# Another order table for a two-stage attention kernel: the same 3969 steps issued in another order, in other banks and buffers

## The chip, the cores and the metric

The kernel runs on one core of one Trainium2 chip. The metric is the device time of one execution in microseconds (us); the program is one launch.

## The reference, cut to what matters

Stage one is clustered attention over 4 batches of 8 heads, 768 positions, 64 values a head. Each query and each key belongs to the nearest of 16 centroids, and a query sees only the keys of its own cluster. Stage two takes the result as x (4 x 768 x 512), and runs causal attention with 4 experts of 64 values each; of an expert's output each token takes the share that its gate gives to that expert if it is one of the token's best two.

```
mask = q_assign[:, :, :, None] == k_assign[:, :, None, :]
scores = where(mask, q @ k.T / 8, -1e9);  attn = softmax(scores);  x = attn @ v
for e in range(4):
    a = softmax(causal((x @ wq[e]) @ (x @ wk[e]).T / 8))
    out += gate_e * (a @ (x @ wv[e]) @ wo[e])
```

## The kernel before

Work is cut into 24 pairs. Pairs 0 to 15 are pairs of heads of stage one, pairs 16 to 23 are pairs of experts of stage two, two for each batch. For each pair the kernel makes operands (`attention_operands` or `moe_operands`), and then runs `core`: scores once to find the maximum of each row (L975 on TensorE, read by VectorE at L983 and L985), the maxima turned into a row (L1001 on TensorE, copied at L1007, placed by a small transfer `tq<-mr`), the scores once more, with the maximum taken off, as two matmuls that add up (L1058 and L1059), the exponential on ScalarE (L1064), the weighted sum of values (L1102), and the sums of the exponentials (partial sums on VectorE or GpSimd, L381 and L382, then L1126).

Three sets of operand tiles `tk` and `tq` go round, so that operands are made ahead. Operands reach them by transfers (`put`, `place_rows`), all issued from one queue, SyncE's (SP below; every such instruction has line L369). For a pair of stage one the last of them are the cluster rows (`tq<-rows`, `tk<-rows`), which leave when the step at L607 is done, and the scaled queries: L648 multiplies out the scale on TensorE, VectorE applies it (L660), ScalarE makes the rounded half (L376), and the transfer `tq<-hi` carries it. The first L975 of that pair waits for them.

Before the first three pairs can be filled, GpSimd clears the three sets (`clear_rows`, four memsets each, L464 and L465: steps 64, 246 and 414).

At the start of each batch of stage two, `x_parts` loads x in four parts (`vt<-x` or `vm<-x`), rounds each (`xh`, L376 or L377) and takes the rest (`xl`, L381 or L382). The projections (L761) need all four. The loads of batches 1 to 3 use two buffers `vt` in turn, so a load waits for the `xl` step of the load before it in the same buffer.

What runs when is not decided by these functions: they only list steps. `SEQ` is a table of step numbers, and `run` issues the steps in that order; the letters a, d and p move a step to ScalarE, VectorE or GpSimd, where it has such a second way. `SLOT` says for each tile which buffer it gets, `ps` being the eight banks of TensorE's results.

```
for word in SEQ.split():
    i = int(word.rstrip("adp"))
    o = self.ops[i]
    eng = self.LETTER.get(word[-1], o.eng)
    ...
    o.ways[eng][1]()
```

So each engine, and the SP queue, works through its own steps in the order in which they stand in `SEQ`, and waits at a step until what that step needs is there. Nothing behind it on the same engine or queue gets past.

Steps that the text names, by their number in `SEQ`:
- 40, 49, 222 and others at L513: loads of q, k and v; 2274 and 2265 are the q and k of pair 13, 1945 the v of pair 11
- pair 0 and 1: 44 (a rounding rest on GpSimd), 260 (scaled queries, `tq<-xl`), 248 and 247 (cluster rows)
- pair 12: 2131 (the second L648), 2135 (`tq<-hi`), 2167 (first L975)
- pair 15: 2630 (the second L648), 2688 and 2643 (L975 of that pair)
- batch 2 of stage two: 3370, 3373, 3376, 3379 (the four loads), 3372 and 3375 (`xl` of the first two), 3377 (`xh` of the third), 3240 and 3241 (`tq<-hi`), 3242 (`tq<-lo`), 3385 (an L761 step that needs all four parts)
- the end: 3935 (sums, L893 and L895), 3894 and 3937 (L908), 3925 (L1102)

The table also holds 37 steps (0 to 36) of two matmuls without use, which stand in the first 20 us.

Of the kernel before, what the change touches and what calls it, by code (L numbers as in the profile page):

```python
# [10 lines left out]
def _warn_once_fixed(msg, *args, **kwargs):  # L11
# [34 lines left out]
422 310 195 268 145 306 177 184 423p 307 196 271 308 185 191 309 263 200 192 272 186 426 264 300 207 187 428 427p  # L46
311 288 189 303 180 190 175 289 202 181 429 269 301 197 203 182 270 208 292 265 183 205 293 261 198 298 188 266 285
201 277 281 206 286 559 283 278 296 560 251 279 273 282 194 193d 274 199 299 297 294 570 284 275 571 210 276 204 561
295 312 280 287 209 211 313 468 563 314d 469 456 315 462 476 457 568 572 441 564d 458 569 178 430 459 212 463 573
179d 477 574 330 442 565 320 213 470 584 445 335 471 353 446 336 575 354 349 576 734 331 332 350 322 214 321 363  # L50
566p 325 364 453 355 323 454 562p 464 318 356 577 351 333 316 326 466 465 358 317 337 319 370 215 359 324 578 338
586 437 579 342 371 438 460 352 451 360 467 343 580 452 361 443 357 585 439 581 327 440 373 328 444 472 587 374 433
473 907 365 329 340 434 366 583 449 447 461 341 474 368 588 725 435 478 369 450 375 582 362 591 431 589 432 376 378
592 436 334 593 448 216 217 590 595 455 475 345 594 596 367d 479 372 480 379d 339 346 481 627 639 482 635 628 483
618 735 636 612 730 736 597 377 640 737 731 619 602 643 732 726 644 738 598 629 218 727 526 603 344 538 728 613 495
527 630 488 539 751 600 599 616 489 610 625 631 611 641 493 642 404 740 494 617 929 347 626 741 380 601 219 381 620
632 614 496 623 742 348 624 528 220 382 637 615 521 638 604 729p 498 522 605 519 499 543 621 520 733p 536 743 523
537 508 524 645 541 509 606 383 529 517 744 542 533 753 518 503 544 531 646 525 484 532 745 752 504 608 746 486 485
633 747 534 634 500 530 748 490 607 510 750 609 758 934 511 647 622 754 938 491 384 505 535 487 755 648 385 546 506
759 760 649 492d 756 501 762 761 935d 497d 650 513 757 749 502d 763 540d 507d 386 547d 512d 514 787 739 651 810 790  # L60
652 695 791 675 696 788 806 930 936 807 665 931 1096 792 811 771 932 775 892 939 666 388 776 800 676 705 764 772 940
767 657 545 706 768 808 653 658 801 783 688 906 793 690 689 784 802 955 941 691 809 773 654 667 774 662 942d 798 956
677 663 803 655 678 708 799 668 794 804 656 670 795 1105 709 779 659 777 671 781 660 778 765 780 672 661 785 796 673
786 515 664 548 797 944 766 782 945 769 812 549d 686 387 770 946 687 805 680 516 937p 947 550 933p 813 957 814 948
789 551 949 815 700 950 816 710 681d 817 701 951 669d 684 952 703 1101 711 953 958 674 704 698 959 962 893 693 963
1097 389 694 824 552 685 839 964d 960 827 692d 840 822 966 820 825 862 828 965 823 697d 863 954 821 1098d 961p 699
713 967 702d 553 707 968 714d 1016 842 1017 1012 221 832 843 679 1013 994 1102 1004 844 995 833 985 1099 1005 834
1103 979 829 845 980 712 1123 991 1014 830 855 1015 875 856 992 983 818 876 904 986 973 835 1104p 996 1108 984 1263
1106 1109 997 870 554 819 998 1107d 987 871 853 826 988 975 872 999 977 851 978 682 852 974 715 873 1111 683d 716
976 854 717 831d 877 1112 969 857 970 1008 1010 858 1444 1002 1113 1011 989 556 971 1009 1006 837 1114 838 847 1100p  # L70
878 836 1124 990 1007 1115 1122 555 1003 972 859 1116 1272 981 1117 1000 865 982 1118 993 867 1001 1119 860 841 1018
1268 1121 861 1125 1019 848 1129 1020d 1120 866 1130 868 880 1126 1021 1131d 1127 718 1132 864d 1133 1128 869d 1041
943 874d 1048 1042 1057 1269 1273 719 879 1058 1031 881d 720 1049 1026 1038 1134 1027 1022 1032 1064 1274 846d 1161
1046 1023 1135 1076 1065 1181 1039 1024 1182 1047 1055 1162 1275 1077 721 1173 1025 1059 1174 1167 1036 1060 1168
1165 1276 1071 1166 1056 1152 1264 1072 1153 1169 1148 1266 1430 1033 1270d 1265 1138 1170 1043 1290 1034 1271p 1028
1149 1037 1278 1044 1029 882 1289 1279 723 849 883d 1139 850 1150 1142 1280 1151 1267p 1136 884 1179 1281 1144 1051
1030 1145 1143 722 1282 1035 885 1180 1137 1291 1154 1283 1155 1183 1061 1284 1146 1069 1062 1184 1439 1285 1147
1063 1158 1286 1079 1159 1163 1081 1070 1287 1052d 1292 1080 1296 1164 1066 1082 1288 1074 1293 1067 1431 1297 1075
1171 1068 1175 1294 1177 1172 1140 1298 1156 1432d 1435 1300 1084 1157 1176 1299p 1178 1301 1185 886 1295p 1141 1160
1073 887 1085d 1186 1442 1187 1040 1440 1188 1443 1350 1305 1441d 1436 1340 1336 1306 1346 1437 1445 1351 1433 1078  # L80
1347 1456 1446 1334 1338 1341 1315 1191 1337 1215 1192 1335 1313 1083 1213 1302 1339 1210 1214 1447 1314 1216 1243
1316 1211 1189 888 1448 1319 1045 1317 1190 1228 1244 1233 1229 1200 1110 1246 1201 1449 557 1231 1050 1234 1193
1457 1205 1194 1318 1203 1247 1224 1204 1450 1438p 1226 1225 1451 1238 1206 1320 1303 1232 1325 1434p 1241 1304 1239
# [136 lines left out]
    vt="011011110101010100101001010101",  # L220
    mx="0110100110100101101010010110100101010101",
# [1071 lines left out]
```

## Time and profile before

| | |
|---|---|
| median of three executions | 693.67 us |
| lowest and highest | 691.22 and 694.33 us |
| profiled execution: its own time | 696.02 us |
| profiled execution: span, first to last instruction | 694.3 us |
| mean granted TensorE clock | 0.997 of full speed |

Busy time is a share of the span. The span is 1.7 us shorter than the time of the execution. The profiled execution is 2.35 us above the median.

### The profile page before, as it was taken

Reading aid. Unit: us, or ns where it says so; the run is one execution under the profiler, and the core shown is the slowest. Engines: PE = TensorE matmul, PEld = TensorE weight load, DVE = VectorE, ACT = ScalarE, POOL = GpSimd, SP = SyncE. Lnnn points to the kernel's source line nnn. Section 1 sums busy time; section 2 is a strip of 40 time slices with the busy share of each in tenths; the row PEclk is TensorE's granted clock in tenths of the full one; section 3 lists DMA queues with packets and bytes.
Section 4 is the critical chain, followed back from the end, with each engine's and each line's share of the span. In section 5 each row is a group of like instructions: output and inputs, shape, how many; then the busy total and the mean of one; then the engine's idle time right before and its main releaser. Section 6 shows DMA issues by size and latency. Waiting matters only on the chain.

```text
span 694.3 us, 13123 instructions
## 1 busy us (share of the span) xinstructions
PE 678.3 (98%) x4529; PEld 526.0 (76%) x4529; DVE 537.1 (77%) x1216; ACT 348.4 (50%) x866; POOL 337.0 (49%) x283
## 2 busy tenths in 40 slices
PE   7999999999999999999999999999999999999997
PEld 5767677767767767757767688779868988887776
DVE  7988899899889798889898865875766476567643
ACT  4646466545646646647656632543443245233542
POOL 4776755555866685664798552110323424122321
PEclk9999999999999999999999999999999999999999
DMA  7876668667696569687778455535664455543323
GB/s 212 203 177 142 162 172 191 167 171 186 162 230 181 148 185 210 154 203 173 175 179 233 123 145 142 143 106 130 171 139 116 115 141 174 139 100 94 115 86 122
DMA packets 78238, 109.64 MB, mean 158 GB/s; under 512 B 22448, under 2 KB 61788, under 8 KB 78172
## 3 DMA queue, kind: packets, MB, share of 16 engines
q1 hardware_dynamic: 78028, 108.78, 61.9%
q8 instruction: 36, 0.59, 0.4%
q14 instruction: 30, 0.25, 0.1%
q10 hardware_dynamic: 144, 0.03, 0.0%
HBM read 36.54 MB, written 12.91 MB: 71 GB/s over the span
## 4 chain that ended last, share of the span: by engine, by line
PE 81%; DVE 6%; DMA 6%; issue 3%; POOL 2%; ACT 2%; SPq 1%; DVEq 0%; ACTq 0%; POOLq 0%
PE ps L1102 18%; PE ps L975 12%; PE ps L1058 12%; PE ps L1059 11%; PE ps L761 10%; PE ps L813 5%; PE ps L1216 4%; PE ps L528 2%; PE ps L1126 2%; DVE mx L985 2%; DMA vt<-x 2%; DMA tq<-hi 1%; PE ps L559 1%; DVE oh L579 1%; PE ps L648 1%
## 5 line engine op out<-in xcount | busy, mean ns | idle before, releaser
L985 DVE TENSOR_REDUCE mx<-ps 128x1 f32<-128x384 f32 (+1 forms) x416 | 209.1, 547 | 29.7 <-PE ps L975 27.2
L1058 PE MATMUL ps<-tq,tk 128*128 128x384 f32 (+2 forms) x528 | 177.6, 339 | 1.1 <-DVE M L983 0.9
L1059 PE MATMUL ps<-tq,tk 97*128 97x384 f32 (+2 forms) x528 | 173.5, 332 | 0.1
L1064 ACT ACTIVATE p<-ps 128x384 f32<-128x384 f32 (+2 forms) x288 | 118.9, 462 | 84.1 <-PE ps L1059 55.8
L975 PE MATMUL ps<-tk,tq 80*128 80x384 f32 (+3 forms) x512 | 146.8, 352 | 5.3 <-DMA tq<-hi 1.7
L1058 PEld LDWEIGHTS ps<-tq,tk 128*128 128x128 f32 x528 | 100.0, 189 | 10.3 <-issue 3.8
L975 PEld LDWEIGHTS ps<-tk,tq 80*128 80x128 f32 x512 | 90.3, 189 | 20.3 <-issue 6.1
L1059 PEld LDWEIGHTS ps<-tq,tk 97*128 97x128 f32 x528 | 100.3, 190 | 2.3 <-DMA tq<-mr 1.2
L1069 POOL TENSOR_SCALAR_AFFINE_SELECT p<-p 128x256 f32<-128x256 f32 x48 | 20.2, 435 | 102.6 <-ACT p L1064 95.3
L381 POOL TENSOR_TENSOR acc<-acc,p 128x768 f32<-128x768 f32 (+2 forms) x31 | 49.2, 1587 | 40.6 <-DVE acc L382 27.4
L983 DVE CUSTOM_DVE_ANT_0 ps<-ps,tri 128x384 f32<-128x384 f32 (+4 forms) x96 | 47.3, 516 | 23.2 <-PE ps L975 22.2
L1102 PE MATMUL ps<-p,vt 128*64 128x384 f32 x288 | 51.4, 492 | 0.1
L1064 ACT ACTIVATE xl<-ps 128x384 f32<-128x384 f32 x88 | 41.8, 499 | 10.0 <-PE ps L1059 9.4
L1064 ACT ACTIVATE xh<-ps 128x384 f32<-128x384 f32 x80 | 38.6, 498 | 11.9 <-PE ps L1059 11.2
L1177 POOL TENSOR_TENSOR xt<-avu,rb 128x384 f32<-128x384 f32 x26 | 27.2, 1054 | 30.7 <-DMA rb<-rd 25.8
L1102 PE MATMUL ps<-p,vm 128*64 128x384 f32 (+2 forms) x288 | 40.8, 422 | 0.0
L376 ACT ACTIVATE hi<-ps 128x384 fp32r<-128x384 f32 x45 | 21.9, 494 | 33.2 <-PE ps L761 23.1
L382 DVE TENSOR_TENSOR acc<-acc,p 128x768 f32<-128x768 f32 (+2 forms) x39 | 31.8, 816 | 7.4 <-POOL p L1069 3.9
L1102 PEld LDWEIGHTS ps<-p,vt 128*64 128x64 f32 x288 | 19.2, 136 | 24.0 <-issue 21.8
L381 POOL TENSOR_TENSOR lo<-xk,hi 128x384 fp32r<-128x384 f32 x24 | 24.1, 1015 | 17.7 <-DMA tq<-lo 5.6
L376 ACT ACTIVATE avu<-ps 128x384 f32<-128x384 f32 x27 | 13.0, 488 | 39.1 <-PE ps L1102 35.1
L1102 PEld LDWEIGHTS ps<-p,vm 128*64 128x64 f32 x288 | 18.8, 136 | 18.2 <-issue 14.1
(277 smaller groups left out, 1441.3 us busy)
## 6 DMA issues: line engine op xcount, KB each, us to landing
tq<-hi SPq DMA_DIRECT2D x88, 192.0 KB
tk<-hi SPq DMA_DIRECT2D x60, 192.0 KB
tk<-lo SPq DMA_DIRECT2D x46, 192.0 KB
rb<-rd SPq DMA_DIRECT2D x46, 192.0 KB
tq<-lo SPq DMA_DIRECT2D x45, 192.0 KB
vt<-in_v_dram SPq DMA_DIRECT2D x16, 384.0 KB
x<-xt SPq DMA_DIRECT2D x16, 384.0 KB
tk<-hi SPq DMA_DIRECT2D x16, 384.0 KB
```

The costliest lines, as they stand in the source:

```text
L376: return op("act", t_act(n, sbuf), lambda: ACT.activation(dst(), src(), AF.Copy), due, after, use, alt=("dve", t_dve(n), lambda: DVE.tenso ...
L381: ways = [("pool", t_pool(n), lambda: POOL.tensor_tensor(dst(), a(), b(), op=fn)), ("dve", t_dve(n), lambda: DVE.tensor_tensor(dst(), a(), ...
L382: ("dve", t_dve(n), lambda: DVE.tensor_tensor(dst(), a(), b(), op=fn))]
L761: PE.matmul(m()[:, :HW], w_()[:, dc, es], x_[dc]()[:, c], start=(i == 0), stop=(i == 3 * DC - 1))
L813: PE.matmul(m()[:, :NV], x_[dc]()[:, ts], w_()[:, dc, :], start=(i == 0), stop=(i == 3 * DC - 1))
L975: PE.matmul(ps()[:, :w], Q[0:R, 0, h, c * 128:(c + 1) * 128], K[0:R, 0, h, i * w:(i + 1) * w], start=True, stop=True)
L983: DVE.tensor_tensor_reduce(ps()[:, :w], ps()[:, :w], tri[:, 512 - w:], 1.0, -3.0e38, OP.add, OP.max, to)
L985: DVE.tensor_reduce(to, ps()[:, :w], axis=AX.X, op=OP.max)
L1058: PE.matmul(p()[:, o_:HW], K[:, 1, h, ks], Q[:, 1, h, qs], start=True, stop=False)
L1059: PE.matmul(p()[:, o_:HW], K[0:R, 0, h, ks], Q[0:R, 0, h, qs], start=False, stop=True)
L1064: ACT.activation(pt()[:, h, po:po + w], p()[:, o_:HW], AF.Exp, scale=SC)
L1102: PE.matmul(av()[h * 64:(h + 1) * 64, o_:HW], d["vv"](h, kc), pt()[:, h, po:po + HW - o_], start=(kc == 0), stop=(kc == nk - 1), tile_posi ...
```

## The change

Two tables are replaced: `SEQ`, and of `SLOT` the entries `ps`, `vt`, `mx`, `acc`, `xt` and `g`. The old tables came from a search over ten sets of random landing times of the transfers, the new ones from a search over 24. Both hold the same 3969 steps, so each engine's instructions differ only in order and buffer, and where a letter moves a step from one engine to another: VectorE has 962 steps before and 951 after, ScalarE 838 and 832, GpSimd 262 and 279, TensorE 1492 and SP 415 in both. Each table is 165 lines long. These are the lines with the steps that the text names:

```diff
--- before.py
+++ after.py
@@ -35,199 +35,199 @@
 SPINS = 37
 
 SEQ = """
-17 40 7 49 34 222 32 414 231 21 30 45 41 64 50 43 390 46d 47 52 54 42 51 37 53d 10 38 44p 39 55 48 56 2 234 70 57 3
...
-104 241 13 100 94 75p 23 85 29 101 92 27 105 230p 242 558 14 243 400 417 89 402 401 246 102 109 96 403 90 244 97 405
...
-110 253 248 134 112 164 257 173 113 129 132 124 258 407 131 174 146 133 254 150 125 161 260 151 255p 171 135 162 155
-408 172 122 136 259p 147 126 166 247 156 120 157 167 154 419 118 409 158 160 127 236 226p 137 262 121 410 159 138
-411 304 116 119 290 412 250 117 176 413 139 165 123 416 141 140 305 291 415 420 142 421 170 267 424 143 302 144 425
...
-1898 2002 1907 1982 2006 2120 2007 1904 1596 2121 1979 2013 1901 1905 1757 2016 1883 1872 1865 2017 2274 1911 1902
-2003 2127 1884 2131 2122 1987 1912 1876 2132 1973 2265 1985 1877 1971 1998 2133 1919 1999 2134p 2128 1758 2129 1870
-1980 2135 1974 1988 2123 1903d 1886 1759 1875d 2136 1908d 2130 1945 2020 1913 1972 1986 1995 1887d 2021 2167 1880
...
-2485 2626 2406 2381 2634 2630 2394 2478 2635 2509 2625 2392 2410 2631 2636 2402 2258 2479 2397 2632 2412 2386d 2398
...
-2688 2682 2523 2641 2421 2524 2775p 2678 2683 2661 2670 2689 2389 2776 2642 2390 2672 2668 2671 2655 2531 2637p 2779
...
-3081 2762 2961 2974 3086 2959 2763 3373 3089 3087d 2975 2871d 2949 2872d 2887 3090 2963 2883 2895 3088 2892 3092
...
-3001d 3370 3031 3374 3235d 3018 3236 3240 3375 3026 3034 3028 3032 3029 2921 3035 3037 3371 3376 3030d 3241 3372
-3187 3173 3038d 3036 3183 3379 3174 3164 3166 3242 3165 3161 3188 3249 3159 3167 3253 3184 3192 3168 3254 3160 3171
...
-3041 3380 3378 3177 3186 3381 3193 2923 3119 3255 3258 3189 3190 3042 3385 3268 3191 2769 3256 2924 3176d 3199 3382
...
-3920 3918d 3814 3922 3929 3927 3923 3894 3930 3924d 3654 3658 3933 3934 3655 3815 3659 3656 3816d 3935 3657 3660
-3895 3661 3817p 3925 3936 3937 3931 3932 3941 3896 3938 3961 3897 3949 3939 3940 3942 3950 3943d 3965 3951 3944 3957
...
+30 40 34 49 10 222 28 64 231 15 2 41 45 52 47 390 46d 42 50 53 37 51d 7 38 48 43 55 39 67 44p 56 14 234 246 57 70 16
+58 32 227 232 25 399 1 3 68 395 59 391 414 223 11 233d 60 36 61 21 224d 62 23 235d 63 8 6 22 228 66 77 392 71 24 79
...
+405 417 105 245 111 107 114 103 126 86 115 94 248 99 406 256 163 87 247 152 91 164 130 148 153 95 252 168 149 110
+253 132 112 169 127 124 157 113 131 128 173 158 257 407 254 133 166 258 255p 146 129 167 260 155 125 174 136 150 156
+408 394p 120 147 161 151 116 567 171 398p 134 172 160 135 162 154 419 409 121 261 137 138 159 410 290 411 118 122
...
+1595 1900 1892 2274 1906 1893 2016 2124 1857 1907 2117 1973 1869 1896 1874 1894 1858 1914 2102 2265 1897 2118 1974
...
+2123 1865 1998 1915 1876 1980 1905 2002 2122 1883 1877 2003 2127 2012 1884 1945 1971 2128 2131 2126 1919 1903d 2132
+2017 2133 1908d 2129 2135 1972 1995 1870d 1886 2136 1875d 1999 2130p 1920d 2013 2134p 2020 1758 1880 2021 2167 2275
...
+2410 2773 2475 2402 2394 2626 2506 2405 2403 2634 2519 2406 2630 2635 2258 2415 2411 2631 2412 2625 2636 2417 2386d
+2632 2397 2509 2638 2398 2633p 2510 2401 2520 2418 2413 2399d 2639 2416 2420 2774 2496 2521 2404d 2771 2409d 2772
+2522 2643 2670 2523 2678 2421 2524 2682 2659 2775p 2679 2389 2644 2776 2390 2661 2660 2666 2688 2683 2529 2637p 2552
...
+3103 2598d 2890 2822 2891d 2762 2898 3105 2896 2899 2880 2958 3106 2897 2959 2902 2955 2953 2978 2763 2979 3097 3370
+2980d 2903d 2981 2764 3373 2823 3094 3098 3104 3108 2906 3095 2987 2912 2910 3100 3096 2913 3113 2911 3099 3101 2904
...
+3001 3239 2921 3018 3371d 3235 3374 3240 3024d 3028 3034 3026 3236 3032 3029 3242 3035 3037 3030d 3372 3181 3166
+3173 3375 3167 3161 3376 3182 3271 3118 3174 3171 3162 3036d 3164 3379 3159 3272 3165 3249 3119 3185 3160 3168 3250
+3120 3265 3267 2922 3253 3163 3183 3268 3241 3002 3184 3266 3039 3170 3169 3038d 3172 3377 3254 2923 3175 3177 2769
+3186 3378 3380 3251 3273 3190 3252 3003 3192 3040 3381 3255 3191 3187 3041 3198 3176d 3188 3247 3385 3248 3189 2924
...
+3920 3929 3911d 3922 3893 3658 3923 3918d 3654 3924d 3659 3926 3655 3927 3930 3934 3656 3815 3933 3660 3935 3661
+3816 3657 3894 3936 3817 3925 3937 3931 3932d 3957 3895 3949 3938 3896 3941 3939 3897 3940 3953 3942 3950 3943d 3958
...
-    vt="011011110101010100101001010101",
...
+    vt="010010001010101011011010100101",
...
```

## Rows read from the trace of the kernel before

**Rows 1.** The page, busy time: us, share of the span, instructions.

```profile
PE 678.3 (98%) x4529; PEld 526.0 (76%) x4529; DVE 537.1 (77%) x1216; ACT 348.4 (50%) x866; POOL 337.0 (49%) x283
```

**Rows 2.** Waits of TensorE: line <- releaser, us in total, times, longest.

```profile
PE ps L975 <- DMA tq<-hi: 1.7, 2, 1.4
...
PE ps L975 <- DMA tq<-rows: 1.2, 1, 1.2
```

**Rows 3.** Windows of 2 us: busy time of each engine, granted clock, transfers.

```profile
516.00:518.00 2.00, 1.11 (x6) 0.77 (x6) 1.27 (x6) 0.66 (x3) 0.00 (x0) 1.00 1.03 227
520.00:522.00 2.00, 0.26 (x5) 0.13 (x1) 0.52 (x1) 1.40 (x3) 0.03 (x1) 1.00 0.08 19
524.00:526.00 2.00, 2.00 (x8) 2.00 (x7) 0.46 (x3) 0.49 (x1) 0.12 (x1) 0.50 0.78 191
```

**Rows 4.** Chain of work, 500 to 526 us: start, us, what.

```profile
507.06 3.63 DMA vt<-x
...
512.69 7.89 DMA vt<-x
...
522.88 3.21 PE ps L761 x11
```

**Rows 5.** Timeline, 506 to 516 us, issues of SP: start, us, what.

```profile
508.35 1.18 SPq L369 DMA_DIRECT2D tq<-hi  x2
...
510.20 1.00 SPq L369 DMA_DIRECT2D vt<-x  x1
...
511.25 1.11 SPq L369 DMA_DIRECT2D tq<-hi  x2
...
513.05 1.16 SPq L369 DMA_DIRECT2D tq<-lo  x2
```

**Rows 6.** Timeline, 20 to 39 us: in brackets idle before and its releaser.

```profile
23.20 0.73 POOL L464 MEMSET tk<- 64x768 f32 x1
...
26.08 0.16 DVE L990 TENSOR_REDUCE xt<-mx 128x3 f32<-128x6 f32 x1 [0.53 <-POOL tq L465]
...
31.93 1.26 SPq L369 DMA_DIRECT2D tq<-xl  x2
...
33.28 1.11 SPq L369 DMA_DIRECT2D tq<-rows  x1
```

**Rows 7.** Chain of work, 0 to 45 us.

```profile
9.17 8.88 issue
...
33.28 4.66 DMA tq<-rows
```

**Rows 8.** Timeline, 298 to 311 us: what stands around one wait.

```profile
298.72 1.03 SPq L369 DMA_DIRECT2D qt<-in_q_dram  x1
...
300.44 0.58 SPq L369 DMA_DIRECT2D kt<-in_k_dram  x1
...
302.82 1.26 SPq L369 DMA_DIRECT2D tq<-hi  x2
...
310.67 0.94 PE L975 MATMUL ps<-tk,tq 80*128 80x384 f32 x4 [1.39 <-DMA tq<-hi]
```

**Rows 9.** Chain of work, undisturbed stretches of TensorE, each timed start to start.

```profile
317.16 0.18 PE ps L1058
...
348.52 4.02 PE ps L1102 x24
...
425.24 4.20 PE ps L761 x24
```

**Rows 10.** Timeline, 302 to 307 us: sums on VectorE and GpSimd.

```profile
302.46 1.82 POOL L381 TENSOR_TENSOR acc<-acc,xh 128x768 f32<-128x768 f32 x1
...
303.62 1.47 DVE L382 TENSOR_TENSOR wvh<-wvh,p 128x768 f32<-128x768 f32 x1
...
305.88 0.95 DVE L382 TENSOR_TENSOR wvh<-wvh,p 128x768 f32<-128x768 f32 x1
```

**Rows 11.** Timeline, 678 to 682 us: the last L908.

```profile
681.05 0.87 PE L908 MATMUL ps<-identf,r 128*64 128x128 f32 x12 [0.41 <-DVE r L902]
```

More of the change, by code (lines that the diff above doesn't have):

```diff
@@ L48 @@
[L48 to L82, printed above, removed]
@@ new lines @@
+548 797 944 813 515 772 664 945 780 677 769 803 946 678 765 814 516 680 766 549 388 550 770 947 387 904 669 389 948
+789 681 949 815 710 950 816 700 674d 817 951 693 952 684 698 694 953 962 703 699 963 958 906 1097 704 959 839 685
+954 832 964d 960 862 692 840 966 822 711 851 863 820 701 713 852 1105 965p 821 551 833 823 967 697d 1098 961 679d
+968 702 714d 991 994 829 995 975 855 992 844 856 552 707 1012 1004 830 875 1013 553 845 1101 976 876 985 824 1005
+1099 1016 973 825 870 1017 842 1100p 554 986 871 1014 853 843 1015 983 712 979 854 974 1106 1102 827 984 1107 998
@@ new lines @@
+1025 1162 1264 1274 943 1057 1023 1265d 1026 1032 1266d 1059 1027 846 1169 1055 1058 1170 1152 1033 1153 1167 1181
+1034 1028 1182 1060 721 1275 1267p 1069 1168 1276 1148 1165 1056 1278 1430 1070 1029 849 1279d 1270 882 1030 850
+883d 1043 1149 884 1046 1044 1183 1166 1146 1047 1142 1138 1147 1035 1280 1444 1136 1143 1061 1281 1439 1036 1150
+1037 1290 1051 1062 723 1151 1271p 1289 1282 1040 1184 885 1139 1137 1291 1283 722 1154 1284 1071 1144 1285 1072
+1045 1145 1171 1286 1140 1081 1141 1163 1287 1066 1082 1155 1296 1179 1067 1164 1079 1288 1050 1052 1074 1297 1080
@@ new lines @@
+2853 2936 2831 2812 2849 2854 2591 2817 2589 2590 2834 2698 3073 2709 2592d 2699 2700 2832 2710 2837 2848 2719 2783
+2851 2694 2701 2852 2705 2695 2850 2855 2737 2706 2702 2838 2843 2818 2711 2703 2856 2712 2721 2844 2704 2714 2857
+2835 2940 2707d 2430d 2937 2941d 2942 2713d 2716 2938 2708 3074 2943 2939 2836 3075 2720 2715 2784 2557 3076 2717
+2722 2724 2944 2718 2723d 2730 2743 2731 2858 2558d 2734 2744 2819 2946 2750 2735 2739 2859d 2732 2947 2740 2860
+2755 3077d 2733 2728 2725 2593 2745 3078 2729 2976 2753 2738 2748 2746 2977 2820 3082 2742 2821 2736d 2741d 2754
@@ L220 @@
-    vt="011011110101010100101001010101",
-    mx="0110100110100101101010010110100101010101",
+    ps="05124326247224670247150307503325634741737266417273615750475714023635634764627112403300167662406112422564"
+       "64355673021446261677733512215120377702136213607322044145770212603161201257206212705551042157320234052401"
+       "37437277653656767311704742012136736510574271230043520333173604526077166740352224474307260453047462505355"
+       "27627227056156266315773206557210142164101647323526560657770740246304553435637633067624343204043035703260"
+       "12401444231053200457473512637461524351412256134755377546500016206621137444605377701030670545615366301165"
+       "40772040323741352131262353272543414420213557575214365465660627343027701536467430225701605076752207122646"
+       "13134302426510610614125745266671756151775122337035512016623570760575623272034557570155600373647141575753"
+       "07412665216776132400335341622731642203511260273074662355065544324717677125426107637712575204466501461474"
+       "56442702116265055373037415010561315374173066647500153003450623112423127260342576433125422405412510561237"
+       "73501340201736503760046451275634154567777720020211113570012360224563576014633606016430722121242043347304"
+       "27015623411367673415413767106005373154042571376046754142003727520712726776764624722035357524005261146061"
+       "13536640532210520162312175120705117374523465320071024557063422306355313767311422475436465630137141646062"
+       "17516544020317551732027742551124435122576206570050743171701567402545110655363115346275462251361245752104"
+       "667150102043416537200331426224330356470116104652307235706412",
@@ L229 @@
     lg="0101",
-    g="10230132",
+    g="01320132",
 )
```

264 lines of the change are left out of this document (134 added, 130 removed).

## Prediction

> **What bounds the kernel now.** I read the page first, then the waits of TensorE, the windows around its longest idle stretches, the chain of work through them, and last the timeline there. The page shows TensorE busy for 678.3 of the span's 694.3 us [rows 1], so 16.0 us of idle time is all that an order can win outright, a little more if stretches at the lower clock go with it. TensorE's work is the same in both tables. The question is therefore which of its waits go, and which new ones come.
>
> The list of waits names few that are long. Transfers are behind them: `tq<-hi` ended two waits of 1.7 us together, the longer 1.4 us, and `tq<-rows` one of 1.2 us [rows 2]. The largest loss stands at 516 to 526 us. TensorE is idle for 0.89 us of the window at 516 and for 1.74 us of that at 520, and at 524 us the granted clock is 0.50, the lower of its two levels [rows 3]. The chain there shows what was late: one load `vt<-x` of 3.63 us, casts, and then another of 7.89 us, from 512.69 to 520.58 [rows 4]. Behind the idle stretch 11 matmuls of L761 take 3.21 us [rows 4], where 24 take 4.20 us undisturbed, 0.175 us each [rows 9]: 3.21 - 11 x 0.175 = 1.28 us lost to the clock. The place costs 0.89 + 1.74 + 1.28 = 3.9 us.
>
> The second place is the head. `tq<-rows` is issued at 33.28 and lands 4.66 us later [rows 6, 7], and TensorE waits 1.2 us for it [rows 2].
>
> **The change, part by part.** *Loads of batch 2.* Before, step 3370 stands late: three TensorE steps behind it comes 3376. The fourth load, 3379, goes into the same buffer as 3370's and must wait until 3370 has landed, been rounded, and had its rest taken: 507.06 to 512.69 [rows 4]. In front of it and beside it SP issues `tq<-hi` twice, the third load and `tq<-lo` [rows 5]. That makes five transfers or pairs of 384 KB from 508.35 to 520.58, at 12.23 / 5 = 2.45 us each. After, 57 TensorE steps stand between 3370 and 3376. The first two loads have long landed, so nothing of the last two hangs on a landing. The queue order after is 3240, 3242, 3376, 3379, and only later 3241: the fourth load ends four such transfers, not five. Worked out from those rows, it lands 2.45 us earlier, which covers the 1.74 us wait and with it the clock loss. Step 3377 also moves from VectorE to ScalarE, so VectorE no longer stands at a cast that waits for the third load while the maxima behind it are due (the 0.89 us). Not everything goes: 3385 stands 18 TensorE steps behind 3379, where it stood 21 behind. I take 3.3 of the 3.9 us; the bounds are nothing (transfers as slow as before) and 3.9.
>
> *The head.* Before, step 247, the rows of pair 1, stands behind 260 in the queue, and 260 waits for the scaled queries until 31.93; 247 leaves only at 33.28 [rows 6]. After, 248 and 247 both stand ahead of 260, so the last to leave is 260 itself, 1.35 us earlier. That is more than the wait of 1.2 us. Also, the clearing 246 stood where GpSimd and VectorE are busy: its four memsets, the first at 23.20 of 0.73 us, end in a wait of VectorE of 0.53 us [rows 6]. After, 246 stands right behind 44, in the 8.88 us in which GpSimd has nothing to do [rows 7]. I take 1.3 us; the bounds are nothing (260 lands as late as 247 did) and 1.2 + 0.5 = 1.7.
>
> *The end.* L908 waits 0.41 us for step 3935's sums [rows 11]. After, 3894 and 3925 stand between 3935 and 3937, where there was only 3925, and 12 more short matmuls cover the wait: 0.4 us, bounds 0 and 0.4.
>
> *Room for the scaled queries.* This part costs. In front of the first L975 of a pair stands only so much TensorE work behind its second L648. For pair 15 that is 14 matmuls of 0.18 us and one L1102 block of 4.02 us [rows 9], 6.5 us; after, 9 matmuls and the block, 5.6. Counted the same way pair 13 goes from 6.4 to 6.0, pair 11 from 7.1 to 5.8, pair 7 from 7.0 to 6.1, pair 14 from 6.5 to 6.3. Before, only two of these waits are seen at all [rows 2], so 6.4 us was enough for most; whether 5.6 is, no row shows. If just 6.4 are needed, the five lose 0.8 + 0.4 + 0.6 + 0.3 + 0.1 = 2.2 us; if 5.6, nothing. I take 1.0, in the middle, as no row is nearer to one end. Should they be as late as pair 12 was, at 1.39 us each [rows 8], it is 7.0.
>
> *Pair 12.* There `tq<-hi` waited behind the loads of pair 13, issued at 298.72 and 300.44, and left at 302.82 [rows 8]. After, those loads (2274, 2265) stand earlier, but 1945, as large, moves in front of 2135, and the room shrinks by seven matmuls of 0.18 us, 1.3 us. I take no change; bounds 1.4 us won, 1.3 lost.
>
> *Other moves.* Eleven steps fewer on VectorE and six fewer on ScalarE, 17 more on GpSimd. TensorE changes between its tile shapes 150 times in place of 151. Both I cost at nothing: what hides the moves is TensorE's own queue of work, and the rival on the port below says what it costs if that cover is gone. The banks are reused after about as much TensorE work as before (half of the 1404 reuses under 2.1 us in both tables, by the same counting).
>
> The sum, against the profiled execution: 696.0 - 3.3 - 1.3 - 0.4 + 1.0 = 692.0 us. That execution is 2.35 us above the median, 1.0034 of it; 692.0 / 1.0034 = 689.7 us, 0.6% under the median of 693.67. Runs of this kernel differ by some tenths of a percent, and about 0.5%, 3.5 us, can be told from no change.
>
> **Rivals.** *The waits are those of one execution.* Landings differ from run to run, and the three runs span 3.1 us. If the loss at 516 us is large only in the profiled execution, the median has little of it to give back; head and end win 1.7, the rooms cost 1.0: 693.67 - 0.7 = 693.0 us, no change. For it speaks that the profiled execution is the slowest of the four; against it, that the fourth load hangs on a landing by the order itself, in every execution.
>
> *The queries come late.* If the shorter rooms of the five pairs wait as pair 12 did, 7.0 us come in, and with 1.7 us won the time is 693.67 + 5.3 = 699.0 us. It ends slower by over 0.5% once the five waits are over 1.0 us each. For it speaks that pair 12 waited with over 9 us of room; against it, that there two loads were just ahead in the queue, and pair 13 made do with 6.4.
>
> *GpSimd holds VectorE up.* A sum on VectorE that began at 303.62 while GpSimd was in a sum until 304.28 took 1.47 us, the next one alone 0.95 [rows 10]. So a clash costs 0.52 us. If each of the 17 steps more on GpSimd brings a clash and TensorE pays all of it for want of free banks, that is 8.8 us, less the 5.0 won above: 697.5 us. It decides from a cost of 0.5 us a step that reaches TensorE; against it, VectorE has eleven steps fewer, and TensorE's long waits are for transfers.
> The Trainium skill, page "SBUF — State Buffer", section "SBUF: two separate sides", says that GpSimd and a VectorE instruction with two SBUF inputs share one pair of ports as a lock, held for a whole instruction. By that rule, which speaks against moving steps to GpSimd, each clash could cost up to the rest of the GpSimd step; the row agrees, as the delayed sum ends 0.8 us behind GpSimd's.
>
> **How the numbers follow.** The forecast has 0.45, the waits of one execution 0.38, the late queries 0.12, the port 0.05. Faster by over 0.5% therefore 0.45, within it 0.38, slower 0.17. For the low end all gains reach their bounds and pair 12's wait goes too: 696.0 - 3.9 - 1.7 - 0.4 - 1.4 = 688.6, or 686.3 on the median's scale. The high end takes in no change and the first part of the late queries, 696.0; above it about 0.13 is left out, below it 0.07.
>
> **What would show it right or wrong.** In the trace after: no idle TensorE over 1 us and no half clock where the projections of batch 2 begin; the last two loads of x issued without an `xl` in between; no wait for `tq<-rows` before 45 us; the memsets of the second and third set before 18 us. New waits of L975 on `tq<-hi` in pairs 7, 11, 13, 15 would show the late queries; many sums of VectorE near 1.5 us the port. The prediction is wrong if the fourth load is as late as before for want of bandwidth, or if waits appear at places that were quiet.

## Result, and the profile after

The change made the kernel slower: 700.19 us median of 9 runs (695.56 to 706.29) beside 693.67 (691.22 to 696.80, 9 runs), a ratio of 1.0084 with a 95% interval of 1.0061 to 1.0107. The forecast was 689.7 us and faster; the range ended at 696.0. The profiled execution after took 698.86 us, of which the span is 696.9.

The page after, its line of busy times (us, share, instructions):

```profile
PE 679.6 (98%) x4529; PEld 525.5 (75%) x4529; DVE 527.6 (76%) x1205; ACT 347.4 (50%) x860; POOL 366.1 (53%) x300
```

TensorE is busy for 679.6 us where it was for 678.3 [rows 1]: 1.3 us of the 2.6 us by which the span grew are matmuls that took longer, the other 1.3 us are idle time, 17.3 for 16.0 us. GpSimd has 29 us more to do and VectorE 9.5 less, as the letters in the table say.

The waits of TensorE after (us in total, times, longest):

```profile
PE ps L1126 <- ACT p L1064: 1.4, 1, 1.4
...
PE ps L1102 <- DMA vt<-in_v_dram: 1.1, 1, 1.1
...
PE ps L975 <- DVE avu L377: 0.8, 1, 0.8
...
PE ps L1058 <- DVE M L983: 0.5, 1, 0.5
...
PE ps L975 <- DMA tq<-hi: 0.2, 1, 0.2
```

`tq<-hi` is down from 1.7 to 0.2 us and `tq<-rows`, 1.2 us before [rows 2], is gone from the list, and so is L908's wait [rows 11]. The first three lines are new. A wait of L1058 for M stood in the list before too, 0.9 us in the window at 516 [rows 3]; that one is gone, and the one shown is at 557 us. The windows of 2 us after show the first place of the forecast, and then a new one (the columns are those of [rows 3]: length, PE, PEld, DVE, ACT, POOL, granted clock, DMA share, GB/s):

```profile
516.00:518.00 2.00, 2.00 (x25) 1.25 (x25) 1.97 (x8) 1.16 (x4) 0.97 (x3) 1.00 1.03 368
518.00:520.00 2.00, 1.70 (x13) 0.73 (x10) 1.69 (x4) 2.00 (x6) 1.33 (x2) 1.00 0.94 290
...
524.00:526.00 2.00, 2.00 (x14) 2.00 (x13) 1.11 (x2) 0.00 (x0) 0.11 (x1) 1.00 0.41 107
...
556.00:558.00 2.00, 1.49 (x20) 0.88 (x19) 1.28 (x6) 1.32 (x4) 0.00 (x0) 1.00 0.99 177
558.00:560.00 2.00, 1.24 (x7) 0.83 (x6) 1.96 (x5) 0.58 (x2) 0.00 (x0) 1.00 0.77 206
560.00:562.00 2.00, 2.00 (x8) 1.66 (x7) 1.70 (x6) 0.00 (x0) 0.00 (x0) 0.62 0.45 92
562.00:564.00 2.00, 2.00 (x7) 1.71 (x7) 0.41 (x2) 0.00 (x0) 0.00 (x0) 0.53 0.44 128
```

At 516 to 526 us the idle time is 0.30 us where it was 2.63, and the clock of 0.50 is gone. At 556 to 560 us there are 1.27 us of new idle time, and the clock falls to 0.62 and 0.53 in the 4 us behind it. A loss of the same kind went away at one place and came at another, 40 us later. (The two new waits come back in six other profiles; the low clock behind them doesn't, see the last section.)

**Three new places.** The first is a load. SP's issues and the chain of work around 391 us, after:

```profile
389.71 1.42 SPq L369 DMA_DIRECT2D vm<-x  x2
391.23 0.38 SPq L369 DMA_DIRECT2D vt<-in_v_dram  x1
```

```profile
391.23 6.02 DMA vt<-in_v_dram
397.25 0.14 issue
397.38 2.16 PE ps L1102 x12
```

Step 2446, the v of pair 14, leaves behind two other loads of 384 KB, takes 6.02 us, and L1102 of that pair waits 1.1 us for it. Counted over the undisturbed times of the TensorE steps in between, the old table has it 22.6 us ahead of that L1102, the new one 4.6.

The second is an order on VectorE. The timeline after, 556 to 560 us (in brackets idle before, and its releaser):

```profile
556.02 0.86 PE L1126 MATMUL ps<-acc,ones 128*32 128x192 f32 x16
556.67 0.42 ACT L376 ACTIVATE acc<-p 128x256 f32<-128x256 f32 x1 [2.02 <-PE ps L1126]
556.72 0.69 DVE L382 TENSOR_TENSOR acc<-p,p 128x512 f32<-128x512 f32 x1 [2.08 <-PE ps L1126]
...
557.73 0.44 PE L1058 MATMUL ps<-tq,tk 128*128 128x384 f32 x1 [0.51 <-DVE M L983]
...
559.67 0.54 PE L975 MATMUL ps<-tk,tq 80*128 80x256 f32 x2 [0.76 <-DVE avu L377]
```

ScalarE and VectorE both stand 2 us at a sum `acc` whose buffer the L1126 of TensorE still has to read. Behind VectorE's sum (3289) stand two steps M and the copy `avu`; they were ready, and TensorE waits for them as soon as its L1126 is through. Each engine takes its steps in the order of the table, so a step that waits for TensorE holds back steps that TensorE waits for.

The third is 25 us later, an order on ScalarE:

```profile
581.45 1.58 ACT L376 ACTIVATE xh<-vt 128x768 fp32r<-128x768 f32 x2 [1.63 <-DMA vt<-x]
582.93 1.23 ACT L1064 ACTIVATE p<-ps 128x384 f32<-128x384 f32 x3
583.55 0.53 PE L1126 MATMUL ps<-acc,ones 128*32 128x192 f32 x8 [1.44 <-ACT p L1064]
```

ScalarE stands 1.63 us at the rounding of a part of x that has not landed, then rounds two parts, and only then does the steps p for which TensorE's L1126 has waited 1.44 us.

### The profile page after: what moved, and what is told of

It reads as the page before. It is cut to its first block, busy times and chain, and to the rows that moved or that the text cites. A ratio compares the mean times of both kernels' runs of the same rounds, so it can differ in the third digit from the quotient of the medians.

```text
span 696.9 us, 13143 instructions
## 1 busy us (share of the span) xinstructions
PE 679.6 (98%) x4529; PEld 525.5 (75%) x4529; DVE 527.6 (76%) x1205; ACT 347.4 (50%) x860; POOL 366.1 (53%) x300
## 4 chain that ended last, share of the span: by engine, by line
PE 79%; DVE 9%; DMA 7%; ACT 1%; issue 1%; POOL 1%; SPq 0%; DVEq 0%; ACTq 0%; POOLq 0%
PE ps L1102 18%; PE ps L975 11%; PE ps L1058 11%; PE ps L1059 11%; PE ps L761 10%; PE ps L813 5%; PE ps L1216 5%; DMA tq<-mr 2%; DVE mx L985 2%; PE ps L528 2%; PE ps L1126 2%; PE ps L559 1%; DVE oh L579 1%; DMA tk<-lo 1%; DMA vt<-x 1%
## 5 line engine op out<-in xcount | busy, mean ns | idle before, releaser
L1058 PE MATMUL ps<-tq,tk 128*128 128x384 f32 (+1 forms) x528 | 178.7, 341 | 0.8 <-DVE M L983 0.5
L1059 PE MATMUL ps<-tq,tk 97*128 97x384 f32 (+1 forms) x528 | 174.1, 333 | 1.2 <-DMA tq<-mr 0.9
L975 PE MATMUL ps<-tk,tq 80*128 80x384 f32 (+4 forms) x512 | 147.2, 351 | 2.6 <-issue 0.8
L1058 PEld LDWEIGHTS ps<-tq,tk 128*128 128x128 f32 x528 | 100.2, 190 | 11.7 <-issue 3.9
L975 PEld LDWEIGHTS ps<-tk,tq 80*128 80x128 f32 x512 | 90.5, 190 | 14.1 <-issue 6.2
L381 POOL TENSOR_TENSOR acc<-acc,p 128x768 f32<-128x768 f32 (+2 forms) x37 | 61.1, 1651 | 54.6 <-ACT p L1064 22.1
L1069 POOL TENSOR_SCALAR_AFFINE_SELECT p<-p 128x256 f32<-128x256 f32 x48 | 21.6, 466 | 103.5 <-ACT p L1064 84.2
L1102 PE MATMUL ps<-p,vt 128*64 128x384 f32 x288 | 51.5, 492 | 1.1 <-DMA vt<-in_v_dram 1.1
L376 ACT ACTIVATE hi<-ps 128x384 fp32r<-128x384 f32 x41 | 19.9, 492 | 47.6 <-PE ps L761 39.3
L1102 PE MATMUL ps<-p,vm 128*64 128x384 f32 (+2 forms) x288 | 41.0, 422 | 0.6 <-POOL p L1069 0.6
L1102 PEld LDWEIGHTS ps<-p,vt 128*64 128x64 f32 x288 | 19.6, 136 | 25.1 <-issue 20.6
L382 DVE TENSOR_TENSOR acc<-acc,p 128x768 f32<-128x768 f32 (+2 forms) x33 | 26.0, 788 | 14.3 <-POOL p L1069 9.6
L381 POOL TENSOR_TENSOR acc<-p,p 128x768 f32<-128x768 f32 (+1 forms) x11 | 18.5, 1683 | 33.8 <-ACT p L1064 29.5
L376 ACT ACTIVATE avu<-ps 128x384 f32<-128x384 f32 x30 | 14.6, 486 | 38.8 <-PE ps L1102 31.1
L1102 PEld LDWEIGHTS ps<-p,vm 128*64 128x64 f32 x288 | 18.6, 136 | 19.6 <-issue 13.6
```

The costliest lines, as they stand in the source:

```text
L376: return op("act", t_act(n, sbuf), lambda: ACT.activation(dst(), src(), AF.Copy), due, after, use, alt=("dve", t_dve(n), lambda: DVE.tenso ...
L381: ways = [("pool", t_pool(n), lambda: POOL.tensor_tensor(dst(), a(), b(), op=fn)), ("dve", t_dve(n), lambda: DVE.tensor_tensor(dst(), a(), ...
L975: PE.matmul(ps()[:, :w], Q[0:R, 0, h, c * 128:(c + 1) * 128], K[0:R, 0, h, i * w:(i + 1) * w], start=True, stop=True)
L1058: PE.matmul(p()[:, o_:HW], K[:, 1, h, ks], Q[:, 1, h, qs], start=True, stop=False)
L1059: PE.matmul(p()[:, o_:HW], K[0:R, 0, h, ks], Q[0:R, 0, h, qs], start=False, stop=True)
L1102: PE.matmul(av()[h * 64:(h + 1) * 64, o_:HW], d["vv"](h, kc), pt()[:, h, po:po + HW - o_], start=(kc == 0), stop=(kc == nk - 1), tile_posi ...
```

## Experiments

The theory of named places: most of the loss comes from a few steps that the new table puts badly, and goes when these are moved. Its rival, many small losses: the new order is a little worse all along, and what is mended in one place comes back in the next. A table is split at points where no buffer and no dependence crosses the cut; *old* and *new* stand for the two tables, with their slots.

All but e12 were timed against the kernel before on the same chip, whose median there was 693.06 us for e1 to e4, 694.21 for e5 to e8, 694.16 for e9 to e12 and 694.27 for e13.

**e1, the new table again, and e2 to e4, halves of it.**

```python
e2 = new[:2887] + [s for s in old if s not in new[:2887]]   # new to the 449th us of TensorE's work
e3 = old[:2887] + [s for s in new if s not in old[:2887]]   # old to the 449th us
e4 = new[:276]  + [s for s in old if s not in new[:276]]    # new to the 38th us
```

> The new tables once more, unchanged, for a second trace. All theories: 1.005 to 1.011 of the kernel before. Order theory (some steps now stand too close behind what they need): TensorE waits again between 556 and 563 us and between 581 and 584 us, where the trace of after lost about 5 us. Landing theory (the waits are where transfers happen to be late): the long waits stand at other places than in the first trace.

> The first 2887 steps in the new order with the new buffers, the rest in the old: new up to some 449 us of TensorE work, old behind. Theory of stage two (the loss is at batch 3, 556 to 584 us): about the old time, 693.7 plus 2.6 us of small waits in stage one less the head's gain, 692 to 697 us, ratio 0.998 to 1.004. Theory of stage one (17 more steps on GpSimd and shorter rooms): all of the loss, ratio 1.008 or more, as the old loss at 516 us comes on top.

> The complement: the first 2887 steps old, the rest new. Theory of stage two: the loss of some 5 us at batch 3 against 4 us won at batch 2, ratio 1.002 to 1.008, with a wide spread from run to run. Theory of stage one: faster than before by the 4 us won at batch 2, ratio 0.994 to 0.998.

> Only the first 276 steps new (38 us of TensorE work), the rest old. If the head gains what I forecast, 1.3 us: ratio 0.998, 0.996 to 1.000. If the waits of the head only move, 1.000.

Measured: e1 700.31 us, 1.0099 (1.0066 to 1.0133); e2 696.67, 1.0044 (1.0018 to 1.0070); e3 699.05, 1.0075 (1.0048 to 1.0101); e4 696.72, 1.0056 (1.0028 to 1.0084). So the loss repeats, and both halves bear a part of it: 0.44 and 0.75% add up to 1.19, beside 0.99 for the whole. A part of that surplus is the cut's own: the profiles of all four tables that change over at the 449th us (e2, e3, and e8 and e13 below) lose about 1 us between the 449th and the 458th us of TensorE's work, by the measure of the stage table below, where no other profile loses more than 0.2. That is some 0.15% of each of the four ratios. e4 tells little of the head: its profile loses about 3 us at 40 to 60 us, just behind the cut, that neither table has by itself. In e1 the chain of work holds the load of pair 14 again, worse:

```profile
390.20 7.18 DMA vt<-in_v_dram
397.38 0.14 issue
397.51 3.46 PE ps L1102 x12
```

The wait is 2.4 us there, and the 12 matmuls behind it take 3.46 us for the 2.16 of the execution above. The granted clock of e1 is 0.55 and 0.59 in the two windows behind the wait, where it is 1.00 in after:

```profile
398.00:400.00 2.00, 2.00 (x10) 0.90 (x7) 0.72 (x1) 0.49 (x1) 1.11 (x1) 0.55 0.03 11
```

In the five profiles with the load at its new place (after, e1, e2, e6, e9) the wait is 1.1, 2.4, 2.1, 1.8 and 3.1 us, 2.1 on the mean; in the ten other profiles, where it stands at its old place or is moved there, there is none.

**e5, the load of pair 14 earlier.** One step is moved ahead on SP's queue, past thirteen issues, among them the loads 2776 and 2779:

```diff
-2530 2534 2671 2446 2540 2535 2414
+2530 2534 2671 2540 2535 2414
...
-2481 2371 2391 2257 2498 2618
+2481 2371 2391 2446 2257 2498 2618
```

> The new table with one step moved: 2446, the load of v for pair 14 (384 KB), stands on SP's queue before step 2257, 18 us of TensorE work earlier, about where the old table has it, and not behind the two loads of xm 2776 and 2779. Theory of named places (most of the loss comes from a few transfers or steps that the new table puts late): in the two profiles of the new table L1102 waits 1.07 and 2.38 us for this load near 391 us, and one of the two loses 1.3 us more to a half clock behind it; so the time falls by 1.1 to 3.8 us, to 696.5 to 699.2 beside 700.3, the ratio to the kernel before to 1.005 to 1.008, and the wait of L1102 for a DMA of vt is gone from the trace. Theory of many small losses (the order is a little worse all along): what is given back here comes back as another wait behind it, and the ratio stays at 1.009 to 1.011.

Measured: 697.19 us, 1.0045 (1.0017 to 1.0072), 0.39 to 0.54% less than the new table's two ratios. The wait of L1102 is gone, as named places would have it. Not all of it is won: this profile has a wait 6 us earlier that the one after has not, for the scaled queries of pair 15:

```profile
391.31 0.41 PE L975 MATMUL ps<-tk,tq 80*128 80x384 f32 x1 [1.07 <-DMA tq<-hi]
```

**e6, batch 3 in the old order, and e7, that and the load of e5.**

```python
h  = new[:3391] + [s for s in old if s not in new[:3391]]   # old behind the 554th us
e6 = h[:3571] + [s for s in new if s not in h[:3571]]       # new again behind the 591st
```

> The new table, but the 180 steps between TensorE's 554th and 591st us (batch 3 of stage two) in the old order, slots with them. Theory of named places: the profiles of the new table lose .51 and .76 us to VectorE at 557 to 560 us, 1.16 more at half clock on the six matmuls of L1216 behind them, and 1.4 us at 582 where L1126 waits for ScalarE; the old order has none of these: 3.8 us less, 696.5 beside 700.3, ratio 1.004 to 1.006. Theory of many small losses: 1.009 to 1.011, with waits of the same sum elsewhere between 554 and 600 us.

> The edits of the two runs before this together: the v load of pair 14 earlier and batch 3 of stage two in the old order. Theory of named places: the two add up, 4.9 to 7.6 us less than the new table, 692.7 to 695.4, ratio 1.000 to 1.003, which leaves the gains at the head and in batch 2 against the small waits of stage one. Theory of many small losses: 1.007 or more.

Measured: e6 700.16 us, 1.0077 (1.0052 to 1.0101); e7 698.76, 1.0066 (1.0032 to 1.0101). By the numbers, many small losses had it right here, and named places had not. The profile of e6 says why. Its waits of TensorE between 550 and 600 us:

```profile
PE ps L975 <- DVE avu L377: 0.8, 1, 0.8
PE ps L1058 <- DVE M L983: 0.5, 1, 0.5
```

The two waits that were to go are still there, to the tenth: the steps that cause them (3289, 3290) stand ahead of the cut. Only the wait for p at 582 us went, and at 610 to 627 us, behind the second cut, three waits of 0.4 to 0.6 us came. The cut missed what it was made for, so the runs don't decide between the two theories.

**e8, the new order in batch 2 alone.**

```python
g  = old[:2887] + [s for s in new if s not in old[:2887]]   # old to the 449th us
e8 = g[:3391] + [s for s in old if s not in g[:3391]]       # and behind the 554th
```

> The old table up to TensorE's 449th us, the new order from there to its 554th (the end of stage one and batch 2 of stage two, with the early loads of x), and the old order behind: the stretch of the predicted gain alone. Theory of the prediction (the loss at 507 to 526 us, 3.3 us and the half clock behind it, is in every execution of the old table): 689 to 690.5 beside 693.1, ratio 0.994 to 0.997. Theory that it was one execution's: the typical execution of the old table does not lose it, so 692.5 to 693.5, ratio 0.999 to 1.001. Theory of many small losses: above 1.002.

Measured: 697.68 us, 1.0042 (1.0021 to 1.0063). The stretch of the forecast gain, put alone into the old table, makes it slower. Its profile has the same two waits for M and `avu`, 0.5 and 0.8 us, since 3289 and 3290 stand in it.

**e9, the sums later.** Two steps are moved past those that TensorE waits for:

```diff
-3297 3179 3216 3290 3289d 3422 3442 3048 3298d 3302 3439 3307
+3297 3179 3216 3422 3442 3048 3298d 3289d 3302 3290 3439 3307
```

> The new table with two steps moved at the border of batch 2 and batch 3 of stage two: 3289 (acc on VectorE) from before its two steps M and the copy avu to behind them, and 3290 (acc on ScalarE) from before a step p to behind it. In the seven profiles so far that hold this border in the new order VectorE stands 2.0 to 2.1 us in step 3289 for L1126 of TensorE, and TensorE then stands .78 and .92 us over its undisturbed times at 556 to 561 us; in one of them the six matmuls of L1216 behind it went at half clock (1.16 us more). Theory of named places: these 1.7 to 2.9 us go, ratio 1.004 to 1.008 where the new table has 1.0084 and 1.0099; the profile has no wait of L1058 for M and none of L975 for avu at 556 to 561 us. Theory of many small losses: the wait goes to another place of batch 3, 1.008 to 1.011.

Measured: 697.06 us, 1.0044 (1.0019 to 1.0069): 0.40 to 0.55% less than the new table, 2.8 to 3.8 us. Windows of e9:

```profile
558.00:560.00 2.00, 2.00 (x26) 1.13 (x29) 1.87 (x7) 0.68 (x2) 0.00 (x0) 1.00 0.26 51
560.00:562.00 2.00, 2.00 (x22) 1.65 (x15) 1.82 (x4) 1.43 (x4) 0.00 (x0) 1.00 0.98 194
562.00:564.00 2.00, 2.00 (x11) 1.72 (x10) 1.61 (x7) 0.00 (x0) 0.00 (x0) 1.00 1.01 263
```

TensorE is busy throughout and the clock stays at 1.00, in these windows and the ones next to them, where the table as it was has 0.76 us idle in the window at 558 and clocks of 0.62 and 0.53. Two steps of 3969 bear about half of the whole loss. The profiles show less of that: two waits of 1.3 us together, 1.9 us by the measure of the stage table (e8 beside e13). The low clock behind them stands in one profile of the seven that have them, and where the rest was lost none shows.

**e10, three places mended.** The load of e5, the sums of e9, and the two roundings of batch 3 with their rests behind three steps p (seven steps in all, not the nine of the expectation):

```diff
-3066 3676 3457 3673 3677 3057 3478 3674 3299 3482 3336 3458 3300d
+3066 3457 3057 3478 3299 3482 3336 3458 3676 3673 3677 3674 3300d
```

> The new table with three places mended, nine steps of 3968 moved: the v load of pair 14 (2446) earlier on SP's queue, the acc steps 3289 and 3290 behind M, avu and p, and the two xh steps of batch 3 (3676, 3673, with their xl 3677, 3674) behind the three p steps 3478, 3482, 3458, since TensorE's L1126 waited 1.0 to 1.5 us for p at 580 to 583 us while ScalarE stood for a load of x. Theory of named places: 3 us for the first (run e5), 1.7 to 2.9 for the second, 1.0 to 1.4 for the third, together 5.7 to 7.3: 693 to 694.5 beside 700.3, ratio 0.999 to 1.002. Theory of many small losses: not under 1.005.

Measured: 695.28 us, 1.0018 (0.9994 to 1.0041). Seven moved steps give back 0.66 to 0.81% of the new table's 0.84 to 0.99%. That is what named places said, and the rival's bound of 1.005 lies outside the interval. The rival keeps a part, though: where the load was moved, another wait came at the first L975 of pair 15, in e10

```profile
388.66 0.41 PE L975 MATMUL ps<-tk,tq 80*128 80x384 f32 x1 [0.98 <-DMA tq<-rows]
```

and 0.4 us for `tq<-hi` behind it, beside the 2.1 us that went. The three shares themselves don't add up: 0.4 or more each for the load and the sums leave next to nothing for the roundings, whose wait of 0.9 to 1.9 us (five profiles) is gone in e10, but followed by one of L761:

```profile
PE ps L761 <- DVE ssb L1134: 0.6, 1, 0.6
```

The intervals, a quarter of a percent either way, allow for that. Which of the first two is worth less than it measured alone stays open.

**e11, the early load alone, and e12, the kernel before once more.** In the old table one step is moved, 3370, the load whose buffer the fourth load waits for:

```diff
-3239 3158 3001d 3370 3031 3374 3235d
+3239 3158 3001d 3031 3374 3235d
...
-3111 2880d 2901 3100 3099 2898
+3111 2880d 2901 3370 3100 3099 2898
```

> The old table with one step moved: 3370, the load of a part of x for batch 2, 24 us of TensorE work earlier on SP's queue, where the new table has it (its buffer is free there). It is the part of the change from which the largest gain was forecast, without the rest. Theory of the prediction (the loss at 507 to 526 us is in every execution): 3.3 us less and the half clock behind it, ratio 0.993 to 0.996. Theory that it was one execution's: 0.999 to 1.001, and the kernel before without that loss in another profile.

> The kernel before once more, for a second profile of it. Theory of the prediction: again 3 us or more of waits for x parts and their followers at 510 to 526 us, with half clock behind, and 1.4 us at 308. Theory that it was one execution's: at most 1 us there, and a time near 692 to 693.

Measured: e11 692.49 us, 0.9974 (0.9952 to 0.9995); e12, one execution, 692.67. The early load by itself is a gain, 1.8 us (0.3 to 3.3), and this kernel is faster than both tables. Beside it e10, which holds the same early load, is 0.44% slower: about 3 us that the three moves don't give back. e12 shows why the gain isn't more. Its waits of TensorE at 500 to 530 us, and the chain through the loads:

```profile
PE ps L975 <- ACT p L1064: 1.4, 1, 1.4
```

```profile
506.52 3.62 DMA vt<-x
...
512.14 6.50 DMA vt<-x
...
520.94 4.20 PE ps L761 x24
```

The order is that of [rows 4], and so is the chain: a load of 3.62 us, and the fourth load behind it at 512.14. But it lands in 6.50 us, not 7.89, TensorE waits 1.4 us, not 2.63, and the 24 matmuls of L761 take 4.20 us, as in an undisturbed stretch [rows 9], with no half clock. In e11 the same two views show

```profile
PE ps L975 <- ACT p L1064: 0.7, 1, 0.7
```

```profile
511.72 6.28 DMA vt<-x
...
520.29 4.20 PE ps L761 x24
```

The fourth load leaves 0.42 us earlier than in e12 and takes 6.28 us: freed of the landing before it, it still has the same transfers around it, since 3241's stay between the last two loads. The wait is halved, not gone.

**e13, e8 with the sums later.** The two steps are moved as in e9.

> The kernel of e8 (old table, with the new order in batch 2 of stage two, TensorE's 449th to 554th us) with the two acc steps 3289 and 3290 moved as in e9. Theory that the acc steps at the end of batch 2 are what made e8 slower: it falls by as much as the new table did in e9 (2.8 to 3.2 us), from 1.0042 to 0.997 to 1.000, near the old table with the early load alone (0.9974). Theory that the new order of batch 2 costs elsewhere too: it stays at 1.002 to 1.005, with waits between 449 and 554 us that the kernel before has not.

Measured: 693.77 us, 1.0005 (0.9980 to 1.0029), 0.37% under e8. No wait of TensorE is left between 550 and 600 us. So most of what made e8 slower were the two sums. Without them the new order of batch 2 is about as fast as the old table, but not as fast as e11, whose early load it holds; about half of those 0.31% is the cut's 1 us, and the rest is not explained.

**Where the time goes, by stage.** For each step of TensorE its time from start to start, less its undisturbed time, added up to the point where 437, 541 and 580 us of undisturbed work are done (the end of stage one, the end of batch 2 just ahead of the two sums, and a little behind batch 3). Undisturbed is the step's time in the first profile of before, and at most 0.15 us above the lower quartile of its kind there. us lost between these points, one profile each:

```
                    0-437   437-541   541-580
before               10.1       6.1       1.0
before, again (e12)   9.3       3.4       1.0
e11                   9.5       2.5       1.0
after                12.2       2.0       6.0
e1                   14.0       3.1       4.3
e9                   15.8       1.9       3.0
e10                  11.9       2.0       1.7
```

The level of a column depends on what is called undisturbed; the differences between rows are what counts. The middle column holds the forecast gain, 4.1 us against the first profile of before and 1.4 us against the second. Over all profiles the ten with the new order of batch 2 lose 2.2 us less there, on the mean, than the four with the old (before, e12, e2, e4). The last holds the sums and the roundings, the first pair 14's load and more: even e10, which doesn't wait for that load, loses 2.4 us more in stage one than e11.

## Why the prediction was wrong

**The step that failed is "Other moves", costed at nothing.** It looked at how many steps change engine and at TensorE's changes of shape, and said that TensorE's queue of work hides the rest. Two of the moved steps that it didn't look at cost most of the loss: the load 2446 of pair 14, with 4.6 us of TensorE's work between it and its user where there had been 22.6 (wait 2.1 us on the mean of five profiles, and a low clock behind it in three), and the sums 3289 and 3290, put ahead of steps that TensorE needs while their own buffer waited for TensorE (2.8 to 3.8 us by e9, 2.6 by e8 and e13; 1.3 us of waits in the profiles). The roundings of batch 3 come on top, with a wait of 0.9 to 1.9 us. The text asked the right question, which waits go and which new ones come, but listed only the first kind, and its own last sign of being wrong, waits at places that were quiet, is what came. The old trace shows the waits that go, and the new ones have to be sought in the new table. Both could be: each load's distance to its user, and each step of VectorE and ScalarE that waits for TensorE with another behind it.

**Loads of batch 2: right in kind, and 3.3 us was too much.** Everything named for the trace is there: no idle TensorE over 1 us and no half clock where batch 2 begins, and the last two loads issued together, without an `xl` in between:

```profile
514.11 1.23 SPq L369 DMA_DIRECT2D vt<-x  x2
```

But the early load alone is worth 1.8 us (e11). The size came from the one execution that was profiled, and that one lost 6.1 us around it where the next lost 3.4. Those 2.7 us are about the 2.35 us by which that execution lies above the median. The sum takes the whole loss off and then divides by 1.0034 for that execution's excess as well, and so counts much of it twice. This was the rival "the waits are those of one execution", and it was half right: the wait is there each time, by the order, and its length differs. The 2.45 us for one transfer fewer ahead of the fourth load came out nearly. In e11, where only the hanging on the landing is taken away, it lands 0.6 us earlier than in e12. With the new order of the queue ScalarE begins to round the fourth part 4.2 to 6.0 us after its issue (ten profiles, 4.9 on the mean), with the old one 6.5 to 7.9 (before, e12, e2, e4; 7.1 on the mean). In after it is issued at 515.01, and its rounding waits for nothing, where e12's waits:

```profile
515.01 0.33 SPq L369 DMA_DIRECT2D vt<-x  x1
...
519.22 0.84 ACT L376 ACTIVATE xh<-vt 128x768 fp32r<-128x768 f32 x1
```

```profile
518.66 0.84 ACT L376 ACTIVATE xh<-vt 128x768 fp32r<-128x768 f32 x1 [2.56 <-DMA vt<-x]
```

**The head: the wait went, most of the gain didn't come.** No `tq<-rows` wait before 45 us, and the memsets of the second and third set stand at 8.64 to 14.24 us, as forecast:

```profile
8.64 0.77 POOL L464 MEMSET tk<- 64x768 f32 x1
...
13.51 0.73 POOL L465 MEMSET tq<- 64x768 f32 x1
```

In seven of the eight profiles with the new stage one, though, the first transposes of `kt` start later and take nearly twice as long (below). By the measure of the table above, at 45 us of undisturbed work these eight have lost 4.6 to 6.2 us, 5.9 on the mean, and the six with the old one 6.0 to 6.4, 6.2 on the mean: 0.3 us won for 1.3 forecast. The two profiles with the new head whose start is not slow, after and e4, do show it: counted to 38 us, where e4's new order ends, they have lost 1.1 us less than the six with the old one, and the other seven 0.3 us more. So the late start goes with the missing gain; what makes it late stays open.

**Pair 12 and the end.** The wait of 1.39 us [rows 8] is gone in after, but in e12 too, with the old order. Of the seven profiles with the old order there, two have such a wait (1.4 us, and 0.9 in e3), of the eight with the new none: it comes and goes, and no change was near the right value. L908's wait is gone as forecast, 0.4 us.

**The rivals.** "The queries come late": `tq<-hi` has 0.2 us of waits after, and 0.2 to 0.6 in the other profiles with the new stage one but e5, where they are 2.4; with the old stage one they are 0.4 to 2.4. So the shorter rooms were enough, and the 1.0 us in the sum was not needed. "GpSimd holds VectorE up" was not tried by itself. The sums of VectorE did get longer in places, `acc<-acc,xh` of 128x768 from 954 to 1266 ns on the mean:

```profile
L382 DVE TENSOR_TENSOR acc<-acc,xh 128x768 f32<-128x768 f32 x10 | 12.7, 1266 | 0.0
```

With three places mended and all letters as they are the kernel is within 0.2% of before, so the clashes can't be the bulk of the loss. Whether they are a part of what e10 still loses against e11 no run shows.

**The sum with the measured terms:** -1.8 (early load), -0.3 (head), -0.4 (end), +0.2 (`tq<-hi`), +2.1 (load of pair 14), +3.2 (sums, the middle of e9's), +1.4 (roundings, mean wait) = +4.4 us. Measured were 0.84 and 0.99%, 5.8 and 6.9 us. Between 1 and 3 us stay open; the column of stage one suggests that they lie there, spread over waits of under 1 us that no run here took apart.

## What to carry to other kernels

A wait seen in a profile says what an order loses in one execution; before it is priced, a second profile of the same kernel should show it at the same length. A new order of the same steps must be searched for its own new waits: for each transfer the work between its issue and its user, and for each engine the steps that wait for the busiest engine and have steps behind them that the busiest engine needs. A table spliced from two has a loss of its own at the splice, about 1 us here, so a profile of it belongs beside its time. A cut for an experiment has to lie ahead of the step that causes a wait, not ahead of the wait: e6, e7 and e8 are read rightly only by the lines that were still there.

## What the runs showed of the hardware that was not expected

A wait of TensorE can cost more than its length. Behind the 2.38 us for the load of pair 14 in e1 the 12 matmuls of L1102 took 3.46 us where they take 2.16 at the full clock. Of the five profiles with this wait, the three in which it is 2.1, 2.4 and 3.1 us have windows at a granted clock of 0.50 to 0.62 behind it, at the lower of the two levels for most of them, and the two in which it is 1.1 and 1.8 us have 1.00. Behind 0.51 and 0.76 us at 557 to 560 us the granted clock fell to 0.62 and 0.53 in after, while in the six other profiles with the same two waits (e1, e3, e5 to e8) it stayed at 1.00. So two executions with the same waits can differ by a us or more. That may be part of why the new table's runs spread over 695.6 to 706.3 us; no run shows it.

At the head the same matmuls took 0.84 us in one execution and 1.51 in another, while the row for the clock said 1.00 in both. The first transposes in e10 and in after, and the window of e10:

```profile
4.76 1.51 PE L528 MATMUL ps<-identf,kt 128*128 128x128 f32 x6 [0.89 <-DMA kt<-in_k_dram]
6.07 1.49 PE L528 MATMUL ps<-identf,qt 128*128 128x128 f32 x6
```

```profile
4.62 0.84 PE L528 MATMUL ps<-identf,kt 128*128 128x128 f32 x6 [0.75 <-DVE nr L429]
```

```profile
5.00:10.00 5.00, 4.95 (x25) 3.17 (x25) 3.90 (x16) 2.69 (x7) 1.14 (x3) 1.00 0.63 217
```

In seven of eight profiles with the new stage one it is 1.51, in the six with the old one 1.51 or 1.52 three times and 0.85 to 0.96 three times. SP issues the first load at 0.81 us in before, after and e10 alike; why `kt` is waited for 0.9 us or more in those seven and 0.35 to 0.54 in the others but after, which waits for VectorE instead, isn't settled, and e4, with the new order of the head, has 0.35.
